# A gated linear-attention and MLP kernel: the vz multiply on GpSimd, one Sigmoid, a group's tail issued one group later, another place for wo

## The chip, the cores and the metric

One core of a Trainium2 chip, bf16 data. The metric is the device time of one execution in microseconds; the median of four runs stands for a kernel.

## What is computed

The sequence has 2048 tokens of 1024 features, the attention 32 heads of 32 features, the MLP 3584 hidden units. The MLP mixes tokens, not features. Cut to its core:

```python
def _A_ref(x, wqkv, w_phi, wo):
    qkv = (x @ wqkv).reshape(B, S, 3, H, Dh)            # q, k, v per head
    pq = einsum("bhsd,hdf->bhsf", q, w_phi)
    pk = einsum("bhsd,hdf->bhsf", k, w_phi)
    phi_q = concat([softmax(pq), softmax(-pq)])         # 64 features
    phi_k = concat([softmax(pk), softmax(-pk)])
    kv  = einsum("bhsf,bhsd->bhfd", phi_k, v)
    z   = einsum("bhsf->bhf", phi_k)
    num = einsum("bhqf,bhfd->bhqd", phi_q, kv)
    den = einsum("bhqf,bhf->bhq", phi_q, z) + 1e-6
    return (num / den) @ wo

def _B_ref(x, w1, b1, w2, b2):
    u = gelu(einsum("bsd,sf->bdf", layernorm(x), w1) + b1)
    return transpose(einsum("bdf,fs->bds", u, w2) + b2)

g = sigmoid((x * gate_w).sum(-1))
out = g * A + (1 - g) * B
```

## The kernel before

The program is written in stages; a scheduler gives each engine's instructions an order from the program order and from free buffers, and each engine then works through its own list in order. A tile pool hands out a fixed number of buffers to each name; a new tile waits until the last reader of the buffer's former tile is done.

**V stage (lines 110 to 133).** x is loaded transposed into xT. For each of 16 token tiles TensorE computes pv (128 tokens by 1024 features of V) and pg (the gate's logit, one column). VectorE and ScalarE (DVE and ACT in the rows) normalise the tile for the MLP (h_tok; the square root of line 126 is on ScalarE), ScalarE casts pv to v_tok (line 132) and makes gate_f from pg by a Sigmoid (line 133). Whenever ScalarE goes from one of these functions to another it loads a table (ACT_TABLE_LOAD).

**Eight groups of four heads (lines 140 to 260).** Each group has 128 of the 1024 columns. Line 153 projects q and k: 64 matmuls of 512 columns, into PSUM tiles pacc (two buffers), copied to qT and kT. Line 166 makes the q features for all tokens, lines 169 and 170 their Exps EpT and EmT (the softmax of q is not divided here, its sums come out of the later product). For two halves tt of the tokens line 177 makes pk, lines 181 and 183 the Exps Ekp and Ekm. For each half and each sign there follow on VectorE: the sum over features Sk (187), its reciprocal rk (190), a cast of rk into the 33rd column of vz (192), and the multiply of v_tok by rk into the other 32 (193). Eight matmuls then add the half's Ek times vz into KVZ (201). Sk, rk and vz have two buffers each. When both signs and halves are in, VectorE masks KVZ to block-diagonal KVbd (207); 32 matmuls (217) multiply EpT and EmT by it, into pM tiles of 128x272, which ScalarE and VectorE move by turns to NB (220, 222). Lines 229 to 248 form the gate chain, here called so: gA, gB, rg, cp, cm (small) and tmp, o_g and their add (128x2048). Sixteen transposes (254) in four pM tiles and four copies (258, 260) put o_g into oT.

The group loop is not pipelined by hand: the scheduler puts a next group's projections between a group's KVZ and pM matmuls.

**Output projection (lines 274 to 290).** wo_sb gets 2 MB by one DMA on ScalarE's queue, into a pool whose memory comes free when the groups' pools are done. For 16 token tiles and two halves of the columns, eight matmuls (pa, line 283) multiply oT by wo_sb; VectorE or ScalarE casts to a_t; a DMA on GpSimd's queue (POOL in the rows) stores it to the output tensor.

**MLP (lines 304 to 356).** First half: 56 x 16 matmuls of pu (319) with weights w1c, in 14 loads on the SP queue, and GELU on ScalarE and VectorE. Second half: 32 x 28 matmuls of pb (344) with weights w2c, loaded on ScalarE's queue; for each tile the bias (348, ScalarE), a load of the stored attention part a_in (350, GpSimd's queue), the mix by gate_f (352, 354, VectorE) and a store (SP).

Of the kernel before, what the change touches and what calls it, by code (L numbers as in the profile page):

```python
# [18 lines left out]
def kernel(ctx, tc, A_x, A_wqkv, A_w_phi, A_wo, B_x, B_w1, B_b1, B_w2, B_b2, gate_w, out):  # L19
# [41 lines left out]
    gate_f = glob.tile([P, NSt], F32, name="gate_f")  # L61
    h_tok = glob.tile([P, NSt, D], BF16, name="h_tok")
# [8 lines left out]
    xT = apool.tile([P, NDt, S], BF16, name="xT")  # L71
# [17 lines left out]
    with tc.tile_pool(name="wvp", bufs=1) as wvp, \  # L89
# [20 lines left out]
        for t in range(NSt):  # L110
# [22 lines left out]
            nc.scalar.activation(gate_f[:, t:t + 1], pg[:], ACT.Sigmoid)  # L133

    with tc.tile_pool(name="grp1", bufs=1) as grp1, \
            tc.tile_pool(name="grp2", bufs=2) as grp2, \
            tc.tile_pool(name="psqk", bufs=2, space=bass.MemoryType.PSUM) as psqk, \
            tc.tile_pool(name="psM", bufs=2, space=bass.MemoryType.PSUM) as psM, \
            tc.tile_pool(name="psg1", bufs=1, space=bass.MemoryType.PSUM) as psg1:
        for g in range(G):  # L140
            load_wqk(g + 2)
            wqg = wq_tiles[g]
            wkg = wk_tiles[g]
            qT = grp1.tile([P, S], BF16, name="qT")
            kT = grp1.tile([P, S], BF16, name="kT")
            for dstT, wg in ((qT, wqg), (kT, wkg)):
                for c0 in range(0, NCH_S, 2):
                    ncl = min(2, NCH_S - c0)
                    pacc = psqk.tile([P, 2, 512], F32, name="pacc")
                    for dt in range(NDt):  # L150
                        for cl in range(ncl):
                            c = c0 + cl
                            nc.tensor.matmul(pacc[:, cl, :], lhsT=wg[:, dt, :],  # L153
                                             rhs=xT[:, dt, ts(c, 512)],
                                             start=(dt == 0), stop=(dt == NDt - 1))
                    for cl in range(ncl):
                        c = c0 + cl
                        nc.scalar.copy(dstT[:, ts(c, 512)], pacc[:, cl, :])  # L158
            EpT = grp1.tile([P, S], BF16, name="EpT")
            EmT = grp1.tile([P, S], BF16, name="EmT")  # L160
            for c0 in range(0, NCH_S, 2):
                ncl = min(2, NCH_S - c0)
                ppq = psqk.tile([P, 2, 512], F32, name="pacc")
# [7 lines left out]
            KVZ = psg1.tile([P, 2, 512], F32, name="KVZ")
            for tt in range(NPK):
                ppk = psqk.tile([P, 2, 512], F32, name="pacc")
                ppk_v = ppk[:].rearrange("p a (b c) -> p (a b) c", c=128)
# [8 lines left out]
                nc.scalar.activation(Ekm[:].rearrange("p a b c -> p (a b c)"),  # L183
                                     ppk_v[:, 0:PKB, :].rearrange("p a b -> p (a b)"), ACT.Exp, scale=-1.0)
                for sign, Ek in ((0, Ekp), (1, Ekm)):
                    Sk = grp2.tile([P, PKB, 4], F32, name="Sk")
                    nc.vector.reduce_sum(Sk[:].rearrange("p a b -> p (a b)"),
                                         Ek[:].rearrange("p a b c -> p (a b) c"), axis=AX.X)
                    rk = grp2.tile([P, PKB, 4, 1], F32, name="rk")
                    nc.vector.reciprocal(rk[:], Sk[:, :, :, None])  # L190
                    vz = grp2.tile([P, PKB, 4, 33], BF16, name="vz")
                    nc.vector.tensor_copy(vz[:, :, :, 32:33], rk[:])
                    nc.vector.tensor_tensor(  # L193
                        out=vz[:, :, :, 0:32],
                        in0=v_tok[:, tt * PKB:(tt + 1) * PKB, g * P:(g + 1) * P].rearrange("p t (j d) -> p t j d", j=4),
                        in1=rk[:].to_broadcast([P, PKB, 4, 32]),
                        op=ALU.mult)
                    for tl in range(PKB):
                        t = tt * PKB + tl
                        lhs = Ek[:, tl, :, :].rearrange("p j d -> p (j d)")  # L200
                        nc.tensor.matmul(KVZ[:, sign, 0:132], lhsT=lhs,  # L201
                                         rhs=vz[:, tl, :, :].rearrange("p j d -> p (j d)"),
                                         start=(t == 0), stop=(t == NSt - 1))
            KVbd = []
            for sign in range(2):
                kb = grp2.tile([P, 136], BF16, name=f"KVbd{sign}")
                nc.vector.tensor_tensor(
                    out=kb[:, 0:132].rearrange("p (j d) -> p j d", j=4),
                    in0=KVZ[:, sign, 0:132].rearrange("p (j d) -> p j d", j=4),
                    in1=blockmask33[:], op=ALU.mult)  # L210
                nc.vector.tensor_copy(kb[:, 132:136], mask4[:])
                KVbd.append(kb)
            NB = grp1.tile([P, NSt, 2, 136], BF16, name="NB")
            for t in range(NSt):
                pM = psM.tile([P, 512], F32, name="pM")
                for sign, ET, off in ((0, EpT, 0), (1, EmT, 136)):
                    nc.tensor.matmul(pM[:, off:off + 136], lhsT=ET[:, ts(t, P)],  # L217
                                     rhs=KVbd[sign][:], start=True, stop=True)
# [168 lines left out]
```

## Time and profile before

| | us |
|---|---|
| median of 4 runs (827.81 to 831.17) | 828.79 |
| the profiled execution | 831.17 |
| its span in the profile | 829.4 |
| TensorE busy | 702.1 |
| VectorE busy | 326.1 |
| ScalarE busy | 329.3 |
| GpSimd busy (almost all of it issuing DMAs) | 45.3 |

The stages by time from the start of the span: load of xT to 44, V stage to 109, groups from 115 to 369, wo_sb and output projection to 436, first half of the MLP to 630, second half to 829. The profile is that of one execution; its engine rows show an operation as output <- inputs, with the line of the kernel, the shape, and how many there were. "Waits" are idle times of an engine just before an instruction, put down to what ended last. The granted clock is a share of TensorE's full 2.4 GHz; it shows 1.00 or 0.50.

### The profile page before, as it was taken

How to read it: one execution, taken by the hardware profiler on the slowest of the kernel's cores; microseconds unless marked ns; L12 is line 12 of the kernel's file. 1: busy time of each engine (PE TensorE's matmuls, PEld its weight loads, DVE VectorE, ACT ScalarE, POOL GpSimd, SP SyncE). 2: the span in 40 equal slices, each digit the busy share in tenths (PEclk: the TensorE clock that was granted, in tenths of full speed). 3: DMA queues.
4: the chain of work that ended last, by engine and by line, in shares of the span. 5: the costliest groups of instructions: out<-in, count | busy, mean ns of one | idle time of the engine just before them, and what ended most of it. 6: DMA issues, size and time to landing. Idle time of an engine off the chain costs nothing.

```text
span 829.4 us, 9250 instructions
## 1 busy us (share of the span) xinstructions
PE 702.1 (85%) x3674; PEld 342.7 (41%) x3744; DVE 326.1 (39%) x597; ACT 329.3 (40%) x522; POOL 45.3 (5%) x84
## 2 busy tenths in 40 slices
PE   0089977797788779437999999999999999999997
PEld 0034433454454445323444444444444444444443
DVE  0135413779678877951222333333332211212121
ACT  0059965645654664420115555555553101111010
POOL 3200000000000000001330000000000100101010
PEclk9999988997897889558999999999999999999999
DMA  9970001100110000019222131313110433544511
GB/s 303 196 163 2 1 0 26 26 14 14 25 26 13 14 1 1 1 29 281 83 77 64 51 101 51 102 52 101 51 51 26 124 92 89 138 129 129 138 39 38
DMA packets 108667, 59.41 MB, mean 72 GB/s; under 512 B 42064, under 2 KB 103504, under 8 KB 108624
## 3 DMA queue, kind: packets, MB, share of 16 engines
q1 hardware_dynamic: 58768, 25.19, 12.5%
q10 hardware_dynamic: 39728, 21.00, 9.6%
q0 software_dynamic: 10128, 12.63, 6.0%
q8 instruction: 29, 0.48, 0.2%
q14 instruction: 14, 0.11, 0.0%
HBM read 46.22 MB, written 8.39 MB: 66 GB/s over the span
## 4 chain that ended last, share of the span: by engine, by line
PE 73%; DVE 5%; ACT 5%; DMA 1%; issue 1%; another core or an unknown queue 0%; DVEq 0%; ACTq 0%
PE pb L344 23%; PE pu L319 23%; PE pacc L153 15%; PE pa L283 7%; PE pM L217 2%; PE KVZ L201 2%; PE pM L254 1%; ACT EmT L170 1%; DMA wo_sb<-in_A_wo_dram 1%; DVE o_g L244 1%; DVE tmp L239 1%; ACT EpT L169 1%; ACT kT L158 1%; DVE o_g L248 1%; ACT Ekm L183 1%
## 5 line engine op out<-in xcount | busy, mean ns | idle before, releaser
L344 PE MATMUL pb<-uTg,w2c 128*128 128x512 bf16 x879 | 192.7, 379 | 2.5 <-ACT S L325 1.6
L319 PE MATMUL pu<-h_tok,w1c 128*128 128x512 bf16 x878 | 192.4, 379 | 1.6 <-ACT a_t L289 0.7
L344 PEld LDWEIGHTS <-w2c 128*128 128x128 bf16 x896 | 87.6, 98 | 107.3 <-issue 1.3
L319 PEld LDWEIGHTS <-w1c 128*128 128x128 bf16 x896 | 87.7, 98 | 106.5 <-issue 1.0
L115 PE MATMUL pv<-Wv,xT 128*128 128x512 bf16 x249 | 62.3, 390 | 46.1 <-DMA xT<-in_A_x_dram 44.3
L348 ACT ACTIVATE bt<-pb,b2f 128x512 bf16<-128x512 f32 x32 | 22.0, 688 | 171.0 <-PE pb L344 166.0
L153 PE MATMUL pacc<-xT,wqg 128*128 128x512 bf16 x242 | 74.1, 446 | 12.6 <-ACT gate_f L133 5.8
L327 DVE SCALAR_TENSOR_TENSOR Pp<-S,U 128x512 bf16<-128x512 bf16 x56 | 38.8, 693 | 96.2 <-ACT S L325 96.2
L352 DVE TENSOR_TENSOR diff<-a_in,bt 128x512 bf16<-128x512 bf16 x32 | 13.6, 425 | 155.0 <-ACT bt L348 155.0
L153 PE MATMUL pacc<-xT,wkg 128*128 128x512 bf16 x248 | 66.8, 379 | 0.3
L283 PE MATMUL pa<-wo_sb,oT 128*128 128x512 bf16 x250 | 56.3, 384 | 9.9 <-DMA wo_sb<-in_A_wo_dram 9.4
L323 ACT ACTIVATE U<-pu,b1f 128x512 bf16<-128x512 f32 x56 | 38.5, 688 | 47.1 <-PE pu L319 44.7
L330 ACT ACTIVATE Sg<-Pp 128x512 bf16<-128x512 bf16 x56 | 35.2, 629 | 41.7 <-DVE Pp L327 41.7
L153 PEld LDWEIGHTS <-wqg 128*128 128x128 bf16 x256 | 27.9, 113 | 42.0 <-issue 26.4
L115 PEld LDWEIGHTS <-xT 128*128 128x128 bf16 x256 | 18.1, 98 | 64.4 <-DMA xT<-in_A_x_dram 44.3
L283 PEld LDWEIGHTS <-oT 128*128 128x128 bf16 x256 | 25.3, 99 | 40.6 <-DMA wo_sb<-in_A_wo_dram 9.7
L220 ACT CAST NB<-pM 128x272 bf16<-128x272 f32 x64 | 25.0, 390 | 39.9 <-PE pM L217 39.9
L222 DVE CAST NB<-pM 128x272 bf16<-128x272 f32 x64 | 28.3, 442 | 30.2 <-PE pM L217 30.2
L331 DVE TENSOR_TENSOR uTg<-U,Sg 128x512 bf16<-128x512 bf16 x56 | 23.8, 426 | 39.5 <-ACT Sg L330 39.5
L193 DVE TENSOR_TENSOR vz<-v_tok,rk 128x1024 bf16<-128x1024 bf16 x32 | 39.0, 1219 | 0.0
L290 POOL DMA_DIRECT2D out_dram<-a_t x32 | 17.4, 544 | 391.7 <-issue 355.4
L325 ACT ACTIVATE S<-pu,b1k 128x512 bf16<-128x512 f32 x56 | 38.1, 681 | 0.0
(74 smaller groups left out, 656.2 us busy)
## 6 DMA issues: line engine op xcount, KB each, us to landing
w1c<-in_B_w_dram SPq DMA_DIRECT2D x14, 1024.0 KB, 5.7
w2c<-in_B_w_dram ACTq DMA_DIRECT2D x8, 1792.0 KB, 9.2
h_tok<-in_A_x_dram POOLq DMA_DIRECT2D x1, 4096.0 KB, 20.7
out_dram<-a_t POOLq DMA_DIRECT2D x32, 128.0 KB, 2.0
a_in<-out_dram POOLq DMA_DIRECT2D x32, 128.0 KB, 2.6
out_dram<-ot SPq DMA_DIRECT2D x32, 128.0 KB, 2.5
Wv<-in_A_wqkv_dram ACTq DMA_DIRECT2D x1, 2048.0 KB, 13.3
wo_sb<-in_A_wo_dram ACTq DMA_DIRECT2D x1, 2048.0 KB, 9.2
```

The costliest lines, as they stand in the source:

```text
L115: nc.tensor.matmul(pv[:, c, 0:DCW], lhsT=xT[:, dt, ts(t, P)], rhs=Wv[:, dt, c * DCW:(c + 1) * DCW], start=(dt == 0), stop=(dt == NDt - 1))
L153: nc.tensor.matmul(pacc[:, cl, :], lhsT=wg[:, dt, :], rhs=xT[:, dt, ts(c, 512)], start=(dt == 0), stop=(dt == NDt - 1))
L193: nc.vector.tensor_tensor(out=vz[:, :, :, 0:32], in0=v_tok[:, tt * PKB:(tt + 1) * PKB, g * P:(g + 1) * P].rearrange("p t (j d) -> p t j d" ...
L220: nc.scalar.copy(NB[:, t, :, :].rearrange("p a b -> p (a b)"), pM[:, 0:272])
L222: nc.vector.tensor_copy(NB[:, t, :, :].rearrange("p a b -> p (a b)"), pM[:, 0:272])
L283: nc.tensor.matmul(pa[:], lhsT=oT[:, g, ts(t, P)], rhs=wo_sb[:, g, ts(c, DCW)], start=(g == 0), stop=(g == G - 1))
L319: nc.tensor.matmul(pu[:], lhsT=w1c[:, t, fl, :], rhs=h_tok[:, t, c * DCW:(c + 1) * DCW], start=(t == 0), stop=(t == NSt - 1))
L323: nc.scalar.activation(U[:], pu[:], ACT.Identity, bias=b1f[:, ft:ft + 1], scale=1.0)
L325: nc.scalar.activation(S3[:], pu[:], ACT.Square, bias=b1k[:, ft:ft + 1], scale=GELU_SK)
L327: nc.vector.scalar_tensor_tensor(out=Pp[:], in0=S3[:], scalar=1.0, in1=U[:], op0=ALU.add, op1=ALU.mult)
L330: nc.scalar.activation(Sg[:], Pp[:], ACT.Sigmoid, scale=GELU_SIG_SCALE)
L344: nc.tensor.matmul(pb[:], lhsT=w2c[:, ft, tl, :], rhs=uTg[:, ft, c * DCW:(c + 1) * DCW], start=(ft == 0), stop=(ft == NFt - 1))
```

## The change

1. The gate's logits are copied from PSUM by VectorE into one tile glogit, and one Sigmoid of 128x16 follows the V loop.
2. In a group, the cast into vz's 33rd column becomes a second reciprocal that writes bf16; the multiply goes from VectorE to GpSimd.
3. What follows o_g in a group (the add, the transposes, the copies to oT) becomes a function, tail. For all groups but the last it is called in the next group, and its instructions are ordered behind that group's last k-feature matmul and last k Exp.
4. In the last group the gate chain and the add are done in four chunks of four token tiles, and the output projection stands inside tail: after each chunk's copy to oT come its 64 matmuls. The PSUM pools of the projections and KVZ are given back ahead of pM, for the pa tiles.
5. wo_sb takes xT's memory (one tag, xwo) and is loaded in two halves, on the SP queue and on ScalarE's.
6. The output projection's stores go from GpSimd's queue to SP, the loads of a_in from GpSimd's to ScalarE's.

The core of the diff:

```diff
-            nc.scalar.activation(gate_f[:, t:t + 1], pg[:], ACT.Sigmoid)
+            nc.vector.tensor_copy(glogit[:, t:t + 1], pg[:])
+        nc.scalar.activation(gate_f[:], glogit[:], ACT.Sigmoid)
...
+            if tt == NPK - 1 and pending is not None:
+                with tc.issue_after(mm_k.ins), tc.issue_after(ex_k.ins):
+                    pending()
+                pending = None
...
-                    nc.vector.tensor_copy(vz[:, :, :, 32:33], rk[:])
-                    nc.vector.tensor_tensor(
+                with nc.allow_low_precision(reason="the rounding of the cast"):
+                    nc.vector.reciprocal(vz[:, :, :, 32:33], Sk[:, :, :, None])
+                nc.gpsimd.tensor_tensor(
...
+        if last:
+            psg1_cm.__exit__(None, None, None)
+            psqk_cm.__exit__(None, None, None)
+            wo_sb = apool.tile([P, NDt, D], BF16, name="wo_sb", tag="xwo")
+            nc.sync.dma_start(out=wo_sb[:, 0:NDt // 2, :],
+                              in_=A_wo[0:(D // 2), :].rearrange("(g p) n -> p g n", p=P))
+            nc.scalar.dma_start(out=wo_sb[:, NDt // 2:NDt, :],
+                                in_=A_wo[(D // 2):D, :].rearrange("(g p) n -> p g n", p=P))
+            asb = g_ctx.enter_context(tc.tile_pool(name="asb", bufs=3))
+            psW = g_ctx.enter_context(tc.tile_pool(name="psW", bufs=3, space=bass.MemoryType.PSUM))
...
+        CH = 4 if last else NSt
+        for lo in range(0, NSt, CH):
+            hi = lo + CH
...
+            if last:
+                nc.vector.tensor_tensor(out=o_g[:, lo:hi], in0=o_g[:, lo:hi], in1=tmp[:, lo:hi], op=ALU.add)
+        def tail(gt=g, o_g=o_g, tmp=tmp, last=last):
+            if not last:
+                nc.vector.tensor_tensor(out=o_g[:], in0=o_g[:], in1=tmp[:], op=ALU.add)
+            for t4 in range(0, NSt, 4):
...
+                if last:
+                    for ti in range(nt):
...
+                            nc.sync.dma_start(out=out_flat[ts(t, P), c * DCW:(c + 1) * DCW], in_=a_t[:])
+        if last:
+            tail()
+        else:
+            pending = tail
...
-                    nc.gpsimd.dma_start(out=a_t[:], in_=out_flat[ts(t, P), c * DCW:(c + 1) * DCW])
+                    nc.scalar.dma_start(out=a_t[:], in_=out_flat[ts(t, P), c * DCW:(c + 1) * DCW])
```

Three places of the engines' lists. The first is VectorE's list in a middle group; Sk is the sum, rk and vz as above, TENSOR_TENSOR on vz the multiply. Before:

```order
L187 TENSOR_REDUCE Sk<-Ekp 128x32
L192 CAST vz<-rk 128x32
L193 TENSOR_TENSOR vz<-v_tok,rk 128x32x32
L190 RECIPROCAL rk<-Sk 128x32
L187 TENSOR_REDUCE Sk<-Ekm 128x32
```

Now, from the last group's add on (lines are those of the changed kernel):

```order
L281 TENSOR_TENSOR o_g<-o_g,tmp 128x2048
L291 COPY oT<-pM 128x512
L201 TENSOR_REDUCE Sk<-Ekp 128x32
L201 TENSOR_REDUCE Sk<-Ekm 128x32
L204 RECIPROCAL rk<-Sk 128x32
L207 RECIPROCAL vz<-Sk 128x32
```

The multiplies between the sums are gone, a copy to oT stands ahead of the sums, and both sums stand ahead of the first reciprocal; a second pair of reciprocals follows, then the other copy to oT and the other half of the tokens in the same order.

The second is TensorE's list where a middle group's pM matmuls end. Before, the next group's q features follow:

```order
L217 LDWEIGHTS EpT
L217 MATMUL pM<-KVbd_1266,EpT 128x136
L217 LDWEIGHTS EmT
L217 MATMUL pM<-KVbd_1269,EmT 128x136
L166 LDWEIGHTS Wbd
L166 MATMUL pacc<-qT,Wbd 128x512
```

Now:

```order
L243 LDWEIGHTS EpT
L243 MATMUL pM<-KVbd_1268,EpT 128x136
L243 LDWEIGHTS EmT
L243 MATMUL pM<-KVbd_1271,EmT 128x136
L163 LDWEIGHTS wkg
L163 MATMUL pacc<-xT,wkg 128x512
```

Fourteen (in some groups 13 or 16) of the next group's k projections stand behind pM that stood ahead of it or in it.

The third is TensorE's list in the last group, where it first reads wo_sb. Before, this is behind the last transposes:

```order
L254 MATMUL pM<-ident,o_g 128x128
L254 LDWEIGHTS o_g
L254 MATMUL pM<-ident,o_g 128x128
L283 LDWEIGHTS oT
L283 MATMUL pa<-wo_sb,oT 128x512
```

Now it is behind the former group's transposes, and the first KVZ matmul follows:

```order
L300 MATMUL pa<-wo_sb,oT 128x512
L300 LDWEIGHTS oT
L300 MATMUL pa<-wo_sb,oT 128x512
L216 LDWEIGHTS Ekp
L216 MATMUL KVZ<-vz,Ekp 128x132
```

Five pa matmuls stand ahead of the first KVZ; 21 in all stand ahead of the last group's own transposes, three more ahead of its last eight of them.

## Rows read from the trace of the kernel before

**Rows 1.** Windows: us, busy of PE, PEld, DVE, ACT, POOL, then clock, DMA, GB/s.

```profile
164.00:194.00 30.00, 24.22 (x169) 14.17 (x169) 23.96 (x41) 17.71 (x29) 0.00 (x0) 0.84 0.08 19
...
338.00:369.40 31.40, 14.08 (x96) 10.11 (x96) 24.40 (x41) 5.80 (x14) 0.00 (x0) 0.50 0.00 1
...
435.60:630.40 194.80, 192.44 (x878) 87.68 (x896) 61.53 (x110) 106.66 (x169) 0.54 (x1) 1.00 0.25 67
```

**Rows 2.** TensorE's waits: for what, us in total, times, longest us.

```profile
PE pacc L177 <- ACT EmT L170: 21.3, 16, 2.7
PE pM L254 <- DVE o_g L248: 14.9, 4, 8.0
PE pa L283 <- DMA wo_sb<-in_A_wo_dram: 9.4, 1, 9.4
...
PE pacc L153 <- ACT gate_f L133: 5.8, 1, 5.8
...
PE KVZ L201 <- DVE vz L193: 4.2, 4, 1.8
```

**Rows 3.** Timeline around groups: start us, us, engine, line, operation, out<-in.

```profile
130.37 0.59 PE L166 MATMUL pacc<-qT,Wbd 128*128 128x512 bf16 x2
...
178.58 0.63 PE L201 MATMUL KVZ<-vz,Ekm 128*128 128x132 bf16 x8
...
179.69 0.22 PE L217 MATMUL pM<-KVbd,EpT 128*128 128x136 bf16 x1
...
186.47 0.59 PE L166 MATMUL pacc<-qT,Wbd 128*128 128x512 bf16 x2
...
191.55 1.08 ACT L181 ACTIVATE Ekp<-pacc 128x1024 bf16<-128x1024 f32 x1
...
329.57 0.59 PE L166 MATMUL pacc<-qT,Wbd 128*128 128x512 bf16 x2
```

**Rows 4.** Timeline at the V stage's end.

```profile
108.62 0.17 PE L118 MATMUL pg<-gw,xT 128*128 128x1 bf16 x1
...
111.99 1.05 ACT L132 CAST v_tok<-pv 128x512 bf16<-128x512 f32 x2
...
114.58 9.05 PE L153 MATMUL pacc<-xT,wqg 128*128 128x512 bf16 x31 [5.79 <-ACT gate_f L133]
```

**Rows 5.** Groups by line and form: busy us, mean ns of one, idle before.

```profile
L193 DVE TENSOR_TENSOR vz<-v_tok,rk 128x1024 bf16<-128x1024 bf16 x32 | 39.0, 1219 | 0.0
L133 ACT ACT_TABLE_LOAD x16 | 20.5, 1283 | 0.3
...
L187 DVE TENSOR_REDUCE Sk<-Ekp 128x32 f32<-128x1024 bf16 x16 | 19.0, 1189 | 25.2 <-ACT Ekp L181 25.2
...
L190 DVE RECIPROCAL rk<-Sk 128x32 f32<-128x32 f32 x32 | 10.7, 340 | 0.0
...
L258 DVE COPY oT<-pM 128x512 bf16<-128x512 bf16 x16 | 6.7, 420 | 6.8 <-PE pM L254 6.8
```

**Rows 6.** Windows of half a microsecond, columns as in rows 1.

```profile
112.00:112.50 0.50, 0.00 (x0) 0.00 (x0) 0.35 (x2) 0.50 (x3) 0.00 (x0) 0.50 0.00 0
...
119.00:119.50 0.50, 0.50 (x4) 0.22 (x3) 0.00 (x0) 0.00 (x0) 0.00 (x0) 1.00 0.00 0
```

**Rows 7.** Groups by line and form: what GpSimd computes.

```profile
masks.py:199 POOL TENSOR_SCALAR_AFFINE_SELECT ident<-ident 128x128 bf16<-128x128 bf16 x1 | 0.3, 306 | 0.1
masks.py:197 POOL MEMSET ident<- 128x128 bf16 x1 | 0.2, 205 | 0.3 <-POOLq L371 0.3
...
L371 POOL MEMSET const-float32-1.0<- 128x1 f32 x1 | 0.1, 99 | 0.0
```

**Rows 8.** Timeline of the last group and of the MLP's first matmuls.

```profile
337.83 1.09 ACT L183 ACTIVATE Ekm<-pacc 128x1024 bf16<-128x1024 f32 x1
...
436.16 4.05 PE L319 MATMUL pu<-h_tok,w1c 128*128 128x512 bf16 x18 [0.67 <-ACT a_t L289]
```

**Rows 9.** The page's DMA issues: engine, operation, count, KB each, us to landing.

```profile
w1c<-in_B_w_dram SPq DMA_DIRECT2D x14, 1024.0 KB, 5.7
```

More of the change, by code (lines that the diff above doesn't have):

```diff
@@ new lines @@
+    psg1_cm = tc.tile_pool(name="psg1", bufs=1, space=bass.MemoryType.PSUM)
+    psg1 = psg1_cm.__enter__()
+    wo_sb = None
+    psW = None
+    asb = None
+    pending = None
+    for g in range(G):
+        load_wqk(g + 2)
+        wqg = wq_tiles[g]
+        wkg = wk_tiles[g]
+        qT = grp1.tile([P, S], BF16, name="qT")
+        kT = grp1.tile([P, S], BF16, name="kT")
+        for dstT, wg in ((qT, wqg), (kT, wkg)):
+            for c0 in range(0, NCH_S, 2):
+                ncl = min(2, NCH_S - c0)
+                pacc = psqk.tile([P, 2, 512], F32, name="pacc")
+                for dt in range(NDt):
@@ L156 @@
                     for cl in range(ncl):
                         c = c0 + cl
[L158 to L163, printed above, removed]
+                        nc.tensor.matmul(pacc[:, cl, :], lhsT=wg[:, dt, :],
+                                         rhs=xT[:, dt, ts(c, 512)],
+                                         start=(dt == 0), stop=(dt == NDt - 1))
@@ L171 @@
[L171 to L174, printed above, removed]
+                    nc.scalar.copy(dstT[:, ts(c, 512)], pacc[:, cl, :])
+        EpT = grp1.tile([P, S], BF16, name="EpT")
+        EmT = grp1.tile([P, S], BF16, name="EmT")
+        for c0 in range(0, NCH_S, 2):
+            ncl = min(2, NCH_S - c0)
+            ppq = psqk.tile([P, 2, 512], F32, name="pacc")
+            for cl in range(ncl):
+                c = c0 + cl
+                nc.tensor.matmul(ppq[:, cl, :], lhsT=Wbd[:, g, :], rhs=qT[:, ts(c, 512)],
+                                 start=True, stop=True)
+            nve = ncl * 512
+            nc.scalar.activation(EpT[:, c0 * 512:c0 * 512 + nve], ppq[:, 0:ncl, :].rearrange("p a b -> p (a b)"), ACT.Exp, scale=1.0)
+            nc.scalar.activation(EmT[:, c0 * 512:c0 * 512 + nve], ppq[:, 0:ncl, :].rearrange("p a b -> p (a b)"), ACT.Exp, scale=-1.0)
@@ L183 @@
[L183 to L191, printed above, removed]
-                    nc.vector.tensor_copy(vz[:, :, :, 32:33], rk[:])
-                    nc.vector.tensor_tensor(
[L194 to L218, printed above, removed]
-                if t % 2 == 0:
-                    nc.scalar.copy(NB[:, t, :, :].rearrange("p a b -> p (a b)"), pM[:, 0:272])
-                else:
-                    nc.vector.tensor_copy(NB[:, t, :, :].rearrange("p a b -> p (a b)"), pM[:, 0:272])
@@ new lines @@
+        NB = grp1.tile([P, NSt, 2, 136], BF16, name="NB")
+        for t in range(NSt):
+            pM = psM.tile([P, 512], F32, name="pM")
+            for sign, ET, off in ((0, EpT, 0), (1, EmT, 136)):
+                nc.tensor.matmul(pM[:, off:off + 136], lhsT=ET[:, ts(t, P)],
+                                 rhs=KVbd[sign][:], start=True, stop=True)
+            if t % 2 == 0:
+                nc.scalar.copy(NB[:, t, :, :].rearrange("p a b -> p (a b)"), pM[:, 0:272])
+            else:
+                nc.vector.tensor_copy(NB[:, t, :, :].rearrange("p a b -> p (a b)"), pM[:, 0:272])
```

161 lines of the change are left out of this document (86 added, 75 removed).

## The prediction

> **What bounds the kernel now.** I read the busy times by stage first, then TensorE's waits, then the timeline of one group, because the change touches the gate, the eight head groups and the output projection, and leaves the two halves of the MLP alone but for a queue. In the MLP, TensorE is the bound: 192.44 of 194.8 us in the first half, 0.219 us for each of 878 recorded matmuls, at the full granted clock [rows 1]; the second half has the same 896 matmuls. What can be had lies before it. A middle group stretch (164 to 194) has TensorE busy for 24.22 of 30 us and VectorE (DVE) for 23.96, so neither alone is the bound; the last group has 14.08 of 31.4 at half the clock [rows 1]. The waits name the gaps: 5.8 us on the last gate value, 14.9 on the o_g add, 9.4 on wo_sb, 21.3 on the Exps and only 4.2 on vz [rows 2].
>
> The quantity for the groups is the period between the ends of two kT projections, that is between two first matmuls of line 166: (329.57 - 130.37) / 7 = 28.46 us [rows 3]. I call such an instant t0.
>
> **The V stage: -6.8.** Behind its last V matmul, at 108.62 + 0.17, TensorE waits until 114.58 for ScalarE (ACT), which still has casts and Sigmoids of the last tiles, each Sigmoid with a table load of 1283 ns [rows 4, 5]. Afterwards one Sigmoid stands behind all casts, and no matmul reads it; TensorE waits for two casts, 1.05 us together, and starts at about 109.5: -5.1. Second, the granted clock had fallen to 0.50 by 112.0, in that wait, and was 1.00 again at 119.0 [rows 6], so the 64 projections took 130.37 - 114.58 = 15.8 us, against 64 x 0.219 = 14.0 at full clock; without the long wait most of it comes back: -1.7. The 16 small copies on DVE lie beside matmuls. If such a copy, queued behind layernorm work, holds a PSUM buffer, half is lost: -3 to -8.
>
> **The period of a group: 20.9 + 4P.** DVE loses per group four multiplies of 1219 ns; GpSimd (POOL) gets them, at P each [rows 5]. In the trace DVE's reduction for the next half runs beside a finished half's multiply. In the changed order both reductions stand ahead of the first reciprocal, so POOL can't start before them, and its four multiplies follow one another. From t0: the first k Exp ends at 191.55 + 1.08 - 186.47 = 6.2 [rows 3]. The add and the four transposes that the change puts ahead are ready by then, because the pM stage ends earlier (below), but one oT copy stands first on DVE, 0.4; two reductions at 1189 ns, 2.4; a reciprocal, 0.34 [rows 5]; with 0.4 for hand-overs POOL starts at 9.7. Four multiplies, 4P; hand-over 0.2; the last eight KVZ matmuls and the masking until the first pM, 179.69 - 178.58 = 1.1; the pM stage, bound by its evictions, 186.47 - 179.69 = 6.8 [rows 3]. In the present order pM ends the group; in the changed one 14 projection matmuls stand behind it, 14 x 0.219 = 3.1. Sum 9.7 + 4P + 0.2 + 1.1 + 6.8 + 3.1 = 20.9 + 4P. The second reciprocal in place of a cast, and the transposes with their copies, lie beside POOL. The moved tail frees TensorE's wait on o_g, but that time was partly cover for the chain that now runs Exp, Sk, POOL, KVZ, pM.
>
> **P is the unknown.** No row shows POOL computing on two tensors. Its nearest rows at 128 columns: a fill takes 205 ns, a fill of one column 99, so 0.82 ns an element; the mask, which reads one tensor and writes one, takes 306 [rows 7]. From below, P could be DVE's 1.22. From the mask, with its fixed part taken out, (306 - 99) x 8 + 99 = 1.75; unreduced 306 x 8 = 2.45; with half of a fill's rate more for the second read 2.45 + 0.42 = 2.87; with a whole one 3.3. I take 2.4, just under the unreduced mask, which is the nearest operation; the ends 1.22 and 3.3 stay for the range. A page also prices the operation: the Trainium skill, GPSIMD Engine Reference, section 3.1, has a two-tensor add 1.96 times as long as on VectorE; by it P would be an estimated 2.39 and the sum the same; no run here shows it yet.
>
> With P = 2.4 the period is 30.5, 2.04 longer than 28.46; seven times that is +14.3, and group 0 has the Exp table load (1.28) that the formula lacks, less its missing oT copy: +0.9. Together **+15.2**. Each 0.1 us of P is 2.8 us over the seven and 0.2 in the last group: 3.0.
>
> **The last group and the output projection: -16.5.** Now: 436.16 - 329.57 = 106.6 from t0 to the first MLP matmul [rows 3, 8]. Of that 256 output matmuls take 56.1, wo_sb 9.4 and the last a_t 0.7 [rows 2, 8]; 40.4 remain until oT is whole. Afterwards the second half of wo_sb is issued on ACT's queue behind the last k Exp, which ends at 337.83 + 1.09 - 329.57 = 9.35 [rows 8]; a 1024 KB load took 5.7 to land [rows 9], so about 15.5. The fifth pa matmul needs it, and the first KVZ stands behind that matmul. The third multiply on POOL waits for that KVZ to free its vz buffer: 15.5 + 0.7 + 2 x 2.4 + hand-overs and a few pa = 21.4 for the last KVZ; 1.1 and 6.8 more end pM at 29.3. The chain on DVE behind it, 8.0 us of TensorE's wait now [rows 2], runs in four chunks, and 168 of the remaining matmuls stand behind the third: three quarters, 6.0, some 0.8 for more small instructions, 1.6 for transposes and copies: 37.7. Then 232 matmuls, 50.8; 0.9 for their start at the lower clock; 0.7 for a_t: 90.1. Saved: 16.5, made of 9.4 for wo_sb, 5.3 for 24 matmuls done ahead (21 of them before the last transposes) and 1.8. If the load lands 3 us later, the whole follows by 3; if the chunks run mostly inside pM, 3 better.
>
> **Queues: 0.** Output stores move from POOL's queue to SP's, where the two first w1c loads already stand ahead of them; later w1c loads wait for buffers anyway. POOL has no DMA left beside its multiplies. The a_in loads go to ACT's queue, between the bias activations; some stand behind a w2c load that waits for its buffer. A tile of the second half takes 28 matmuls, 6.1 us, so a load late by a few us is covered; if one isn't, DVE's end comes later, not TensorE's, and only the last tile counts, below 1 us.
>
> **Sum.** -6.8 + 15.2 - 16.5 = -8.1. On the profiled run, 831.17 (span 829.4, and 1.8 around it), that is 823.1. That run is the slowest of the four shown; on their median of 828.79 it is 820.7, so **821**.
>
> **Rivals.** (1) *POOL is slower*, and the kernel ends slower than before. The mechanism is the serial chain of four multiplies in each group. It breaks even at P = 2.4 + 8.1 / 30 = 2.67 and is slower by over 0.3% (2.5 us, about what a measurement of this kernel can tell from no change) from 2.75. At 2.87 it gives 835, at 3.3 it gives 848; I say 842. For it: a second operand that is read as a float32 broadcast; against it: the mask's row also computes an index for each element. (2) *POOL is nearly as quick as DVE*, 1.22 to 1.75. Then DVE's own work decides: from 7.2 after t0 it has four reductions, 4 x 1.19, eight reciprocals, 8 x 0.34, and two oT copies, 0.84, which ends at 15.5; the last KVZ comes at about 16.3 and the period is 16.3 + 11 = 27.3. That is 3.2 less than forecast in seven groups, and 2 to 3 in the last: 796. Its row is the 1.75; against it stands that the fixed part of one row must be right. (3) *POOL and DVE hinder each other.* No stretch of the trace has both computing. If each multiply holds off the reciprocals that DVE has queued beside it, the next multiply starts up to 0.34 later, four times a group: 1.2 in seven groups, 8.4: 829, no change. If the second pair of reductions is held off too, another 2.4 a group: 846, on the side of the first rival. The Trainium skill, SBUF — State Buffer, section "Who interferes with whom", says that DVE and GpSimd share one pair of ports under an exclusive lock, which a DVE instruction with two SBUF inputs takes against GpSimd's reads, and one with a single input outside the two-port modes does not. By it the reductions and reciprocals beside POOL are free and the sum stands; only a copy of oT could block. (4) *The clock falls in the groups.* If TensorE's pauses for POOL kept it at half clock through pM and the last projections, 35 matmuls would cost 0.22 more each, 7.7 a group: some 875. Against it: a wait of 5.8 us took the clock down, and it was back at 119.0, soon after the restart at 114.58 [rows 4, 6]; a pause for one multiply is at most P, with matmuls between. (5) That the moved tail doesn't move: by the emitted order it does, so only its worth is open, inside the forecast.
>
> **How the numbers follow.** Forecast, 811 to 826: 0.52. POOL slower, with the worse half of (3): 0.22. POOL quick: 0.12. Mutual hindrance to about no change: 0.10. Clock: 0.04. The forecast's own range is P from 2.1 to 2.57. The 8-in-10 range reaches down to P = 1.75 (821 - 19.5, rounded to 801) and up to P = 2.9 (836). Of the forecast nearly all is faster by over 0.3% (0.50); with 0.12 of (2) and 0.02 of (3) faster is 0.64. Same: 0.02 + 0.07 + 0.04 of (1), 0.13. Slower: 0.23.
>
> **What would show it.** The multiplies' duration on POOL is P; the distance of two first qT-feature matmuls should be 20.9 + 4P, 30.5; in each group KVZ should wait on POOL's vz. The wait on gate_f should be gone and the clock 1.00 over the first projections. wo_sb's wait should go from 9.4 at the projection to a wait of the fifth pa matmul at 15.5 after the last t0; from that t0 to the first MLP matmul should be 90. Wrong would be a period that doesn't follow P, VectorE instructions longer beside POOL, a lower clock behind KVZ, or waits on a_in in the second half.

## The result

The changed kernel takes 796.54 us (median of 10 runs, 795.56 to 802.07) against 829.83 (16 runs, 827.81 to 832.96): ratio 0.9609, 95% interval 0.9593 to 0.9625. That is 33 us saved where 8 were forecast, and below the range of 801 to 836. The profiled execution took 796.00, its span is 794.2; before, 831.17 and 829.4.

The spans differ by 35.2 us, and three instants of TensorE's timeline say where: the first q-feature matmul of group 0 (called t0 of group 0 below), that of group 7, and the first MLP matmul. Columns as in rows 3.

```profile
106.97 7.07 PE L163 MATMUL pacc<-xT,wqg 128*128 128x512 bf16 x31 [1.16 <-ACT v_tok L133]
...
120.78 0.59 PE L176 MATMUL pacc<-qT,Wbd 128*128 128x512 bf16 x2
...
317.82 0.59 PE L176 MATMUL pacc<-qT,Wbd 128*128 128x512 bf16 x2
...
401.03 4.26 PE L354 MATMUL pu<-h_tok,w1c 128*128 128x512 bf16 x18 [0.67 <-ACT a_t L306]
```

| us | before | after | difference | forecast |
|---|---|---|---|---|
| start to t0 of group 0 | 130.37 | 120.78 | -9.6 | -6.8 |
| t0 of group 0 to t0 of group 7 | 199.20 | 197.04 | -2.2 | +15.2 |
| t0 of group 7 to the first MLP matmul | 106.59 | 83.21 | -23.4 | -16.5 |
| the MLP | 393.24 | 393.17 | -0.1 | 0 |

TensorE's waits after the change (for what, total, times, longest), beside rows 2:

```profile
PE pacc L187 <- ACT EmT L180: 20.6, 16, 2.7
PE KVZ L216 <- POOL vz L208: 8.8, 12, 1.0
...
PE pM L287 <- DVE o_g L278: 3.4, 1, 3.4
PE pa L300 <- ACT Ekm L193: 1.6, 1, 1.6
...
PE pacc L163 <- ACT v_tok L133: 1.2, 1, 1.2
```

The waits for gate_f and wo_sb are gone, that on o_g fell from 14.9 to 3.4, and a new one on GpSimd's vz is about 1.1 a group. The wait behind the Exps stays. The unknown of the forecast, and its neighbours on VectorE (busy us, mean ns of one | idle before), beside rows 5:

```profile
L208 POOL TENSOR_TENSOR vz<-v_tok,rk 128x1024 bf16<-128x1024 bf16 x32 | 60.2, 1915 | 246.1 <-DVE rk L204 143.0 <-ACT Ekm L193 103.2
...
L201 DVE TENSOR_REDUCE Sk<-Ekp 128x32 f32<-128x1024 bf16 x16 | 19.3, 1204 | 22.5 <-ACT Ekp L191 22.5
...
L204 DVE RECIPROCAL rk<-Sk 128x32 f32<-128x32 f32 x32 | 10.7, 334 | 2.8 <-POOL vz L208 2.8
```

P was 1.92 for one multiply, not 2.4; four in a row take 7.52, since each starts 1.87 behind the one before. Here is one group of the changed kernel, from its t0 at 150.34 to the next:

```profile
156.55 1.21 DVE L201 TENSOR_REDUCE Sk<-Ekp 128x32 f32<-128x1024 bf16 x1
...
159.29 7.53 POOL L208 TENSOR_TENSOR vz<-v_tok,rk 128x1024 bf16<-128x1024 bf16 x4 [20.49 <-DVE rk L204]
...
166.87 0.63 PE L216 MATMUL KVZ<-vz,Ekm 128*128 128x132 bf16 x8
...
167.98 0.22 PE L243 MATMUL pM<-KVbd,EpT 128*128 128x136 bf16 x1
...
174.78 3.19 PE L163 MATMUL pacc<-xT,wkg 128*128 128x512 bf16 x14
...
177.80 0.59 PE L176 MATMUL pacc<-qT,Wbd 128*128 128x512 bf16 x2
```

Read it against the forecast's terms: GpSimd starts 8.95 after t0 (9.7 forecast), its four multiplies take 7.53 without a gap, KVZ follows at once, 1.1 to the first pM, 6.8 for pM, then 14 projections, 3.0. That adds up to this group's 27.46; 20.9 + 7.52 would be 28.4, and the mean period, with group 0's 29.56 in it, is 28.15.

### The profile page after: what moved, and what is told of

Same layout as the page of the kernel before. It is cut to its first block, busy times and chain, and to the rows that moved or that the text cites. A ratio compares the mean times of both kernels' runs of the same rounds, so it can differ in the third digit from the quotient of the medians.

```text
span 794.2 us, 9291 instructions
## 1 busy us (share of the span) xinstructions
PE 691.0 (87%) x3672; PEld 336.4 (42%) x3744; DVE 293.9 (37%) x608; ACT 289.0 (36%) x478; POOL 70.8 (9%) x52
## 4 chain that ended last, share of the span: by engine, by line
PE 76%; DMA 5%; ACT 5%; issue 4%; POOL 4%; DVE 4%; POOLq 0%; DVEq 0%; ACTq 0%
PE pb L379 24%; PE pu L354 24%; PE pacc L163 9%; PE pv L116 8%; PE pa L300 7%; DMA xT<-in_A_x_dram 5%; POOL vz L208 4%; PE pM L243 2%; ACT EmT L180 2%; ACT EpT L179 1%; DVE Sk L201 1%; DVE o_g L273 1%; DVE tmp L269 1%; ACT kT L168 1%; PE pacc L187 1%
## 5 line engine op out<-in xcount | busy, mean ns | idle before, releaser
L354 PEld LDWEIGHTS <-w1c 128*128 128x128 bf16 x896 | 87.7, 98 | 106.5 <-issue 1.0
L208 POOL TENSOR_TENSOR vz<-v_tok,rk 128x1024 bf16<-128x1024 bf16 x32 | 60.2, 1915 | 246.1 <-DVE rk L204 143.0
L163 PE MATMUL pacc<-xT,wqg 128*128 128x512 bf16 x241 | 68.9, 408 | 3.8 <-issue 1.3
L163 PE MATMUL pacc<-xT,wkg 128*128 128x512 bf16 x249 | 63.2, 379 | 0.3
L300 PE MATMUL pa<-wo_sb,oT 128*128 128x512 bf16 x249 | 59.2, 389 | 2.7 <-ACT Ekm L193 1.6
L116 PEld LDWEIGHTS <-xT 128*128 128x128 bf16 x256 | 16.0, 98 | 60.6 <-DMA xT<-in_A_x_dram 44.3
L163 PEld LDWEIGHTS <-wqg 128*128 128x128 bf16 x256 | 25.6, 106 | 26.4 <-issue 12.4
L163 PEld LDWEIGHTS <-wkg 128*128 128x128 bf16 x256 | 23.1, 98 | 17.4
## 6 DMA issues: line engine op xcount, KB each, us to landing
h_tok<-in_A_x_dram POOLq DMA_DIRECT2D x1, 4096.0 KB, 20.9
Wv<-in_A_wqkv_dram ACTq DMA_DIRECT2D x1, 2048.0 KB, 13.5
```

The source lines that it names most:

```text
L116: nc.tensor.matmul(pv[:, c, 0:DCW], lhsT=xT[:, dt, ts(t, P)], rhs=Wv[:, dt, c * DCW:(c + 1) * DCW], start=(dt == 0), stop=(dt == NDt - 1))
L163: nc.tensor.matmul(pacc[:, cl, :], lhsT=wg[:, dt, :], rhs=xT[:, dt, ts(c, 512)], start=(dt == 0), stop=(dt == NDt - 1))
L208: nc.gpsimd.tensor_tensor(out=vz[:, :, :, 0:32], in0=v_tok[:, tt * PKB:(tt + 1) * PKB, g * P:(g + 1) * P].rearrange("p t (j d) -> p t j d" ...
L300: nc.tensor.matmul(pa[:], lhsT=oT[:, gg, ts(t, P)], rhs=wo_sb[:, gg, ts(c, DCW)], start=(gg == 0), stop=(gg == G - 1))
L354: nc.tensor.matmul(pu[:], lhsT=w1c[:, t, fl, :], rhs=h_tok[:, t, c * DCW:(c + 1) * DCW], start=(t == 0), stop=(t == NSt - 1))
```

## The experiments

Twelve more kernels were run. For each the table has the median and the three parts of the span, taken from the same instants as above; "KVZ" is the start of the last KVZ matmuls after t0, in groups 1 to 6, and "behind pM" the number of the next group's projections that TensorE's list has between pM and the next q features, in groups 0 to 6. The parts are those of one profile.

| kernel | median us | t0 of group 0 | period | last group | KVZ | behind pM |
|---|---|---|---|---|---|---|
| before | 829.83 | 130.37 | 28.46 | 106.6 | 19.8 to 22.0 | 0 to 4 |
| after | 796.54 | 120.78 | 28.15 | 83.2 | 16.5 to 17.6 | 13 to 16 |
| e1, before + gate | 820.32 | 120.20 | 28.30 | 106.5 | 19.7 to 21.6 | as before |
| e2, after, multiply on VectorE | 807.40 | 120.21 | 28.72 | 91.5 | 21.7 to 24.4 | 0 to 2 |
| e3, before + multiply on GpSimd | 836.54 | 129.29 | 29.74 | 103.8 | 16.6 to 19.9 | 16 to 19 |
| e4, after, more work on GpSimd | 810.87 | 119.19 | 30.08 | 85.4 | 18.6 to 20.1 | 9 to 15 |
| e5, after, tail at once | 808.20 | 120.39 | 29.85 | 84.5 | 16.6 to 19.9 | 16 to 19 |
| e6, after, queues back | 796.47 | 119.45 | 28.38 | 83.3 | 16.6 to 17.6 | - |
| e7, after, one chunk | 801.01 | 119.18 | 28.37 | 87.6 | 16.5 to 17.6 | - |
| e8, after, reduction reordered | 798.74 | 120.53 | 28.39 | 84.5 | 16.6 to 17.5 | 12 to 16 |
| e9, after, old projection | 817.17 | 120.49 | 28.55 | 103.6 | 16.5 to 18.0 | - |
| e10, after, half the multiply | 789.58 | 120.44 | 27.33 | 83.6 | 15.0 to 15.7 | 16 to 19 |
| e11, e2 and e5 together | 807.68 | 120.54 | 28.81 | 91.5 | 21.9 to 24.3 | - |
| e12, after, last multiply split | 797.61 | 120.05 | 28.58 | 83.1 | 16.1 to 17.5 | 16 to 18 |

How far a period can be trusted is seen where the seven groups' program is the same: the changed kernel, e6, e7 and e9 have 28.15, 28.38, 28.37 and 28.55, the kernel before and e1 28.46 and 28.30. So the 2.2 us that the groups gained in the first table lie within the spread of single profiles: the groups are about as long as before.

**The gate.**

```diff
-            nc.scalar.activation(gate_f[:, t:t + 1], pg[:], ACT.Sigmoid)
+            nc.vector.tensor_copy(glogit[:, t:t + 1], pg[:])
+        nc.scalar.activation(gate_f[:], glogit[:], ACT.Sigmoid)
```

> The kernel before with the gate part alone: the logits copied by VectorE, one Sigmoid behind the V loop. Theory A, ScalarE's table loads set the pace of the whole V stage (its windows show it busy for 3.94 of every 4.00 us): the V matmuls end 3.0 us earlier, the wait behind them falls by 4.6, the first projections gain 2.0 at the full clock, in all -9.6, 820. Rival, the recorded prediction, only the end of the stage changes: -6.8, 823, with the last V matmul ending at 108.8 as before.

It took 820.32, ratio 0.9883 (0.9866 to 0.9900): -9.5, theory A. The same four microseconds in the middle of the V stage, in the kernel before and then in the changed kernel (us, then busy PE, PEld, DVE, ACT, POOL, clock, DMA, GB/s):

```profile
92.00:96.00 4.00, 3.67 (x24) 1.78 (x24) 2.16 (x6) 3.94 (x7) 0.00 (x0) 1.00 0.00 0
```

```profile
92.00:96.00 4.00, 3.92 (x27) 1.90 (x27) 0.16 (x1) 1.37 (x3) 0.00 (x0) 1.00 0.00 0
```

Before, ScalarE is full (3.94 of 4.00) and TensorE isn't; each tile costs ScalarE two table loads of 1283 ns, two casts and two small functions, some 4.05 us, more than the 3.8 that TensorE takes for one in e1. What TensorE loses by it, some 0.2 us a tile, is easily overlooked: the wait list has it as 1.3 us on v_tok, and as 4.0 us in 14 pieces of the weight loads, put down to "issue". In e1 the V matmuls end at 105.2 instead of 108.8, and the first projection starts at 106.39 (106.97 in the changed kernel), against 114.58 before.

**The multiply on GpSimd: length of the chain.** e4 puts a second multiply of 128x256, which also reads rk, ahead of each multiply:

```diff
+                nc.gpsimd.tensor_tensor(
+                    out=fil[:],
+                    in0=v_tok[:, tt * PKB:tt * PKB + 2, g * P:(g + 1) * P].rearrange("p t (j d) -> p t j d", j=4),
+                    in1=rk[:, 0:2].to_broadcast([P, 2, 4, 32]),
+                    op=ALU.mult)
                 nc.gpsimd.tensor_tensor(
```

> The changed kernel with GpSimd's work made longer: ahead of each multiply a second one of 128x256 into a scratch tile, which also reads rk and so can't run earlier; about 0.5 us each, so that four cost together what four multiplies of the predicted 2.4 us would. Theory A, the period is 20.9 + 4P and P alone was mis-sized: the period rises to about 30.2, the whole by 16 to 812. Rival, something beside GpSimd sets the period: the four fillers are partly hidden, below 804.

It took 810.87 (0.9769, 0.9752 to 0.9785), 14 more than the changed kernel: theory A. The period is 30.08, 1.9 longer than the changed kernel's for 2.3 more on GpSimd; with some 2.46 for a pair of instructions 20.9 + 4P would be 30.7. TensorE's waits on vz, 8.8 in the changed kernel, and the two sizes:

```profile
PE KVZ L222 <- POOL vz L214: 20.9, 23, 1.4
...
L214 POOL TENSOR_TENSOR vz<-v_tok,rk 128x1024 bf16<-128x1024 bf16 x32 | 61.2, 1913 | 0.0
L209 POOL TENSOR_TENSOR fil<-v_tok,rk 128x256 bf16<-128x256 bf16 x32 | 19.7, 616 | 242.8 <-DVE rk L204 140.9 <-ACT Ekm L193 101.9
```

So an element costs (1913 - 616) / 768 = 1.69 ns, and 183 ns are fixed. With P = 2.46 the change would still have been 19 us faster than before; the forecast of 8 wasn't wrong by P alone.

e10 goes the other way. The multiply fills half of the columns; the other half stays zero, in two vz tiles that are cleared once:

```diff
-                    out=vz[:, :, :, 0:32],
+                    out=vz[:, :, :, 0:16],
```

> The changed kernel with half of each multiply left out: GpSimd fills 16 of each head's 32 columns of vz, the rest stays at zero from one memset (so o has zeros there); matmuls keep their shapes. The multiply should take 183 + 512 x 1.69 = 1050 ns, by the two sizes measured. Theory A, 20.9 + 4P also holds downward: 3.4 us less in seven groups and the last, 769. Theory B, TensorE's work and the Exps bound the group: at most 1.1 a group in seven groups, and 3.5 in the last, where nothing else fills TensorE: 785 to 790.

It took 789.58 (0.9511, 0.9484 to 0.9537): 7 less, theory B in the groups. A multiply fell to 1056 ns, but the last KVZ comes only 1.1 to 2.3 us earlier, not 3.4, since GpSimd now waits some 1.3 for VectorE's reductions and reciprocals ahead of its third multiply (the floor that the second rival has, there 16.3). TensorE's waits on GpSimd fell from 8.8 to 0.7 in all, and the period by 0.8. That is about what a quicker GpSimd can give: the wait of 1.1 a group.

The last group didn't gain, against both theories. Its last KVZ comes 0.8 earlier, 15.8 after t0, and its first pa matmul behind its own transposes 1.0 earlier; the 163 pa matmuls that follow lose 1.3 again, because the granted clock stays at half for longer. First e10's wait, this row of matmuls and the clock in its third microsecond, then the latter two in the changed kernel (columns of the window as above):

```profile
PE KVZ L219 <- POOL vz L211: 0.7, 2, 0.3
...
342.97 37.66 PE L303 MATMUL pa<-wo_sb,oT 128*128 128x512 bf16 x163 [0.22 <-issue]
...
345.00:346.00 1.00, 1.00 (x4) 0.33 (x3) 0.00 (x0) 0.18 (x1) 0.00 (x0) 0.50 0.00 0
```

```profile
349.95 36.37 PE L300 MATMUL pa<-wo_sb,oT 128*128 128x512 bf16 x163 [0.22 <-issue]
...
352.00:353.00 1.00, 1.00 (x6) 0.47 (x5) 0.00 (x0) 0.41 (x1) 0.00 (x0) 1.00 0.00 0
```

Both kernels have TensorE waiting 3 us for o_g shortly before, and short bursts between; why the clock came back 3 us later in e10, counted from the start of these matmuls, isn't shown.

**The multiply on VectorE, and the deferred tail.** e2 changes `nc.gpsimd.tensor_tensor` to `nc.vector.tensor_tensor` in the changed kernel; e3 makes part 2 alone in the kernel before; e5 calls the tail in its own group:

```diff
-            pending = tail
+            tail()
```

and e11 does what e2 and e5 do, together.

> The changed kernel with the vz multiply put back on VectorE, all else as changed. Theory A: in the changed order VectorE has, from 7.2 us after t0, four reductions, eight reciprocals, two copies and four multiplies in a row, 13.2 us, so the last KVZ comes at 20.6 instead of 16.6 after t0; the period grows from 28.2 by 3 to 4 us and the time to 822 (815 to 828). Rival: GpSimd's serial chain of 4 x 1.88 is as long as what it replaced, and the move is worth nothing: 797.

> The kernel before with part 2 alone (second reciprocal, multiply on GpSimd). Theory A: the chain Exp, Sk, GpSimd, KVZ, pM is as long as the period before, and the move alone gains little: 825 to 832. Rival: the move carries the groups' gain by itself, 3 us a group or more: 805.

> The changed kernel without part 3: every group's tail is called at once, in its own group. Theory A: the add stands at the same place of VectorE's list either way, so only the place of the transposes and of some projections changes, and what is saved ahead of the k Exps is lost behind pM: within 5 us of 797. Rival: the deferral is what lets the groups gain, 2 us a group or more without it: 812 or above.

> The changed kernel without parts 2's move and 3: multiply on VectorE, each group's tail called at once; gate, wo and projection as changed. Theory A, parts 2 and 3 pay only together: groups as in the kernel before, 28.3 a period, the last group 8 longer than in the changed kernel: 804 to 808, no worse than without either one alone (807, 808). Rival, their gains are independent, each costing some 11 when taken away: 818.

e2: 807.40 (0.9726, 0.9709 to 0.9743), between its two theories. The last KVZ came even later than A had it, up to 24.4, but the period, 28.72, is only 0.2 to 0.6 above those with the multiply on GpSimd, because next to nothing stands behind pM any more (0 to 2 projections, where the changed kernel has 13 to 16), and from group 1 on part of pM itself comes behind the next t0 (at 234.67 the last 14 of its 32 matmuls). TensorE has the same work in either list; a late KVZ is covered by projections, an early one leaves them for later. In the last group there are none to cover with, and the part behind its t0 is 8.3 us longer.

e3: 836.54 (1.0073, 1.0057 to 1.0089): part 2 alone makes the kernel before slower by 7, which neither theory had. e5: 808.20 (0.9737, 0.9715 to 0.9759): without the deferral the changed kernel loses 11.7, more than A and a little less than the rival had it; nearly all of it is period, 29.85. A group of e5, from t0 at 178.98, shows why:

```profile
178.98 0.59 PE L176 MATMUL pacc<-qT,Wbd 128*128 128x512 bf16 x2
...
183.06 1.71 PE L287 MATMUL pM<-ident,o_g 128*128 128x128 bf16 x12 [1.74 <-DVE o_g L281]
...
184.56 1.06 PE L187 MATMUL pacc<-Wbd,kT 128*128 128x128 bf16 x8
...
188.54 1.22 DVE L201 TENSOR_REDUCE Sk<-Ekp 128x32 f32<-128x1024 bf16 x1 [3.31 <-ACT Ekp L191]
...
191.29 7.52 POOL L208 TENSOR_TENSOR vz<-v_tok,rk 128x1024 bf16<-128x1024 bf16 x4 [24.61 <-DVE rk L204]
```

The transposes of the former group stand in TensorE's list ahead of the next group's k features and wait 1.74 for the add; so the k Exps, the reductions and GpSimd start late, GpSimd 12.3 after t0 instead of 9 to 10. Two of e5's groups are like this, and behind every pM 16 to 19 projections are left. The deferral forbids that order.

e11: 807.68 (0.9733, 0.9712 to 0.9755), no worse than e2: theory A. With the multiply on VectorE the deferral is worth nothing; with the tail at once the multiply on GpSimd is worth nothing (808.20). Together they bring 11, of which 8.3 are in the last group.

**wo, the projection, the chunks.** e9 has the old output projection (own pool for wo_sb, one load on ScalarE's queue when the groups are done, all matmuls behind the last transposes, one chunk), e7 only

```diff
-        CH = 4 if last else NSt
+        CH = NSt
```

> The changed kernel without parts 4 and 5: wo_sb in its own pool, loaded in one piece when the groups are done, the output projection behind the groups, the last group's chain in one piece; stores on SP. Theory A: the 9.4 us wait for wo_sb and the 24 matmuls done ahead come back, and the chunks' part, together 19: 815. Rival: the last group's gain is mostly the shorter GpSimd chain, and these parts are worth 8 or less: 804.

> The changed kernel with the last group's gate chain in one piece instead of four chunks; wo, and the projection behind each transpose, as changed. Theory A: the add ends 8 us behind pM and the first output matmuls of this group's oT start some 4 us later: 800 to 802. Rival: VectorE's work is the same in one piece or four, and smaller instructions cost as much as the overlap brings: 796 to 797.5.

e9: 817.17 (0.9852, 0.9830 to 0.9874), so parts 4 and 5 are worth 20.6; e7: 801.01 (0.9670, 0.9635 to 0.9704), so 4.5 of them are the chunks. Both are near theory A.

**The queues.** In e6 the stores and the a_in loads go back to GpSimd's queue:

```diff
-                            nc.sync.dma_start(out=out_flat[ts(t, P), c * DCW:(c + 1) * DCW], in_=a_t[:])
+                            nc.gpsimd.dma_start(out=out_flat[ts(t, P), c * DCW:(c + 1) * DCW], in_=a_t[:])
...
-                    nc.scalar.dma_start(out=a_t[:], in_=out_flat[ts(t, P), c * DCW:(c + 1) * DCW])
+                    nc.gpsimd.dma_start(out=a_t[:], in_=out_flat[ts(t, P), c * DCW:(c + 1) * DCW])
```

> The changed kernel with the output projection's stores and the loads of a_in back on GpSimd's queue. Theory A, the recorded prediction: the queues are worth nothing, 796 to 798. Rival: the store or load queue delays something in the projection or the MLP, or the stores delay w1c on SP in the changed kernel: a difference of 3 us or more in either direction.

796.47 (0.9613, 0.9577 to 0.9650): the queues are worth nothing that can be measured.

**Two tries for a shorter chain.** e8 orders the second reduction of a half behind the first reciprocal; e12 splits a group's last multiply:

```diff
+                with (tc.issue_after(rc.ins) if sign else contextlib.nullcontext()):
-                nc.vector.reduce_sum(Sk[:].rearrange("p a b -> p (a b)"),
+                    nc.vector.reduce_sum(Sk[:].rearrange("p a b -> p (a b)"),
...
-                nc.vector.reciprocal(rk[:], Sk[:, :, :, None])
+                rc = nc.vector.reciprocal(rk[:], Sk[:, :, :, None])
```

> The changed kernel with VectorE's second reduction (sign minus) ordered behind the first reciprocal, so that GpSimd starts one reduction earlier. Theory A, the period is GpSimd's serial chain plus a constant: some 1.2 us a group less, 787. Theory B, TensorE's own work (22.8 of 27.46 us in a group) and its 3.5 us behind the Exps leave at most the 1.1 us that it waits for GpSimd in a group, and what the chain gains is lost in matmuls behind pM: 793 to 799.

```diff
...
+                jn = 2 if tt == NPK - 1 and sign == 1 else 4
+                nc.gpsimd.tensor_tensor(out=vz[:, :, 0:jn, 0:32], in0=v_v[:, :, 0:jn, :],
+                                        in1=r_v[:, :, 0:jn, :], op=ALU.mult)
+                if jn < 4:
+                    nc.vector.tensor_tensor(out=vz[:, :, jn:4, 0:32], in0=v_v[:, :, jn:4, :],
+                                            in1=r_v[:, :, jn:4, :], op=ALU.mult)
```

> The changed kernel with the last of a group's four multiplies split: GpSimd does two of each four heads (1056 ns), VectorE, which is idle there, the other two. Theory B, a group is TensorE's work and its waits for the Exps and for GpSimd, and the last wait goes: up to 0.8 us a group, also in the last, 790 to 793. Rival, the list of TensorE's matmuls, which is laid out anew, loses it again behind pM, as with the reordered reduction: 796 to 799.

e8: 798.74 (0.9624, 0.9604 to 0.9644); GpSimd's first multiply starts some 0.7 earlier, but the second then waits 0.75, put down to its reciprocal or to a KVZ, and the last KVZ comes no earlier. No gain: B. e12: 797.61 (0.9611, 0.9591 to 0.9632), no gain either, and it shows something the changed kernel doesn't, VectorE and GpSimd both multiplying at once:

```profile
L211 POOL TENSOR_TENSOR vz<-v_tok,rk 128x512 bf16<-128x512 bf16 x8 | 12.0, 1505 | 0.0
L214 DVE TENSOR_TENSOR vz<-v_tok,rk 128x512 bf16<-128x512 bf16 x8 | 11.1, 1382 | 0.0
```

GpSimd's half takes 1505 where e10, with only one-input work beside it, has 1056; VectorE's takes 1382 where the last group's chunked tmp, of the same shape, takes 671 (and the whole multiply of the kernel before, twice as large, 1219):

```profile
L272 DVE TENSOR_TENSOR tmp<-NB,cp 128x512 bf16<-128x512 bf16 x4 | 2.7, 671 | 0.0
```

So GpSimd's half takes 0.45 us longer beside the other, VectorE's 0.71. No version that computes the whole result beats the changed kernel.

## Why the prediction was wrong

Of what the kernel saved beyond the forecast, 2.8 us lie in the V stage, 17.4 in the groups and 6.9 in the last group with the output projection. Each has a step of its own that failed; the largest is the size of P.

**The V stage, -9.6 instead of -6.8.** The step that failed is the reading that only the stage's end changes: the prediction prices what TensorE loses behind the last V matmul and puts the stage itself at nothing. A window of a few tiles would have shown ScalarE at 3.94 of 4.00, that is, the stage's bound. Without the loads the V matmuls end 3.0 us earlier (3.6 in e1). The end's own terms came nearly as forecast: the wait went from 5.8 to 1.2 (-4.6, forecast -5.1), the projections, now at full clock, from 15.8 to 13.8 (-2.0, forecast -1.7).

**P, 1.92 instead of 2.4.** The term that failed in the groups is P. With the measured 4P = 7.52 the formula gives 28.4 (28.55 with its extra for group 0); measured are 28.15. It held upward, where e4 added 1.9 to the period for 2.3 more, but not downward, where e10 took 0.8 off for 3.4 less; so its agreement at P = 1.92 suggests that the chain just about binds there. The size of P was wrong, and with it the sign: by the formula 4 x 0.52 x 7 = 14.6 of the 17.4 by which the groups missed, and some 12 if e4's 13.5 for 0.58 more is scaled to 0.52. The rest is an earlier start of GpSimd (9.4 after t0 in the mean of groups 1 to 6) and a shorter hand-over to KVZ, within what single profiles differ by. The mask's row gave both 1.75, with its fixed part taken out, and 2.45 without; that fixed part was measured beside it (99), and scaling it by eight was the mistake, since e4 finds a fixed part of 183 and a slope of 1.69 against the mask's 1.6. So the second input cost little, as far as two operations can be compared. The working also says that in the kernel before a reduction runs beside a finished half's multiply; both stand in VectorE's list, one after the other. No term rests on that. The Trainium skill, GPSIMD Engine Reference, section 3.1, has a factor of 1.96 against VectorE for float32; here, with bf16 v_tok and a float32 rk, it is 1915 / 1219 = 1.57, and the measurement decides.

**The last group, -23.4 instead of -16.5.** The last KVZ came at 16.6 instead of 21.4. About 2 of that are a misread list: I held the fifth pa matmul, ahead of the first KVZ, for one that needs the second half of wo_sb, but by the tile numbers of TensorE's list it is the next tile's first, and it ran before that half had landed (the second of the two from 328.15). The first that need it are the two at 333.06, behind the third KVZ, and the load was issued at 324.24 and landed 5.3 later, at 329.5. Some 2.1 more are P, 4 x 0.52 once nothing waits for wo_sb, and the rest is GpSimd's earlier start, 9.1 after t0:

```profile
324.24 0.38 ACTq L235 DMA_DIRECT2D wo_sb<-in_A_wo_dram  x1
...
326.23 0.69 ACT L293 COPY oT<-pM 128x512 bf16<-128x512 bf16 x1
...
328.15 1.06 PE L300 MATMUL pa<-wo_sb,oT 128*128 128x512 bf16 x2
...
332.60 0.63 PE L216 MATMUL KVZ<-vz,Ekp 128*128 128x132 bf16 x8
...
333.06 0.59 PE L300 MATMUL pa<-wo_sb,oT 128*128 128x512 bf16 x2
...
334.46 0.63 PE L216 MATMUL KVZ<-vz,Ekm 128*128 128x132 bf16 x8 [0.81 <-POOL vz L208]
...
337.62 0.18 DVE L263 TENSOR_TENSOR gA<-NB 128x16 f32<-128x16 bf16 x1
...
342.22 0.32 PE L243 MATMUL pM<-KVbd,EmT 128*128 128x136 bf16 x1
...
347.42 1.46 PE L300 MATMUL pa<-wo_sb,oT 128*128 128x512 bf16 x3 [0.42 <-DVE oT L291]
```

So no wait for wo_sb is left. The load was also issued earlier than the last k Exp's end, 326.4, which I had it wait for. Behind KVZ the chunks did better than forecast: the first one's gate chain begins at 337.62, inside pM, which ends at 342.5, and 4.9 lie between that and the first pa matmul behind this group's own transposes, at 347.42, where the forecast had 8.4; the forecast named this case as 3 better. The output matmuls from there on took 1.2 longer than forecast. With 4.6 by the earlier end of pM these make the 6.9. The parts that I valued (9.4 for wo_sb, 5.3 for 24 matmuls, the chunks) are borne out in their sum by e9 and, for the chunks, by e7.

**The rivals.** The second rival's time, 796, is what was measured, but not for its reason: it wanted P at 1.75 or less and VectorE as the bound, worth 3.2 a group against the forecast; the groups came within some 0.3 of their old length, and the time came from the two other parts. That its number fits is luck. Its floor of VectorE's work appeared only in e10, where the last KVZ stood at 15.0 to 15.7 and the period at 27.33, 27.3 forecast. The third didn't happen in the changed kernel: Sk takes 1204 beside GpSimd against 1189, rk 334 against 340, and GpSimd's multiplies 1908 to 1917 whatever stands beside them. It did happen in e12, where VectorE has two inputs. That two such instructions contend, and one with a single input doesn't, is as the Trainium skill, SBUF — State Buffer, section "Who interferes with whom", has it, and the trace agrees with both halves of it. The fourth didn't: the granted clock over whole groups rose from 0.83 to 0.88 before to mostly 0.94 (in e6, with the same groups, 0.83 to 0.94). The queues cost nothing (e6).

**What the list hides.** That GpSimd frees VectorE of four multiplies, 4.9 us a group, and the groups stay about as long isn't a paradox: the last KVZ comes 3 to 5 us earlier, and 13 to 16 projections, 3.1 us, that used to stand ahead of it stand behind pM. The forecast had that term. TensorE is busy for most of a group, here in the one from 150.34 (columns as in rows 1):

```profile
150.34:177.80 27.46, 22.77 (x162) 12.86 (x164) 18.27 (x36) 15.41 (x26) 7.53 (x4) 0.94 0.09 20
```

Of the other 4.7 us it waits 2.5 for the q Exps, 0.7 for kT and 0.9 for vz. Before, a group has 23.34 of 27.69. So a shorter chain can give back the wait for vz and little else, which e10 bears out; a longer one is paid nearly in full, as e4 shows.

## What to carry to other kernels

Before a removed instruction is priced as a wait at a stage's end, look at a window of the stage's middle: an engine at 98% there sets the pace, even if the wait list has only crumbs for it. Price an unseen operation by a row's slope and fixed part taken apart, and give that price most of the weight. When a stage's work is shared between engines, count how many matmuls an in-order list leaves behind the chain: a shorter chain pays most where nothing else fills the waiting engine, here the last group (e2: 8.3 us for 7.2 on KVZ; the half multiply of e10 paid nothing there, as the clock took its gain); and a moved operation and a moved tail may pay only together, as e3, e5 and e11 show.

## Unexpected of the hardware

ScalarE's list has the load of wo_sb's second half behind two Exps and a copy to oT. It was issued at 324.24, though the copy itself began at 326.23: this DMA start didn't wait for the compute ahead of it to run. One case is shown here; e9's load, behind a freed pool, says nothing on it. And two engines that each multiply two tensors lengthened each other by 0.45 and 0.71 us (e12), while reductions, reciprocals and copies beside GpSimd took as long as before.
